# Attention keys in chunks of 128, 128, 128 and 64, the last chunk on quarters and eighths of TensorE

## The chip, the cores and the metric

One core of a Trainium2 chip. The metric is device time in microseconds (us), the median of a few runs; an interval is 95%. All runs told of here are at a granted TensorE clock of 0.988 to 0.998, where 1 is full speed. A ratio compares the mean times of two kernels' runs of the same rounds, so it isn't quite the ratio of the medians.

## The reference, cut to what matters

```python
# q, k, v: (8, 12, 448, 64) float32: 8 batches, 12 heads, 448 positions, 64 wide
q_n, k_n = rmsnorm(q, g_q), rmsnorm(k, g_k)
attn = softmax(q_n @ k_n.T / 8)            # 448 x 448 per head
x = (attn @ v)                             # -> (3584, 768)
h = x @ w_in                               # 768 -> 2048
out = (h - tanh(h)) @ w_out                # 2048 -> 768
```

The kernel works on pairs of heads: 48 pairs, six to a batch. The products with the weights of batch b run between the attention of batch b + 1, on the same TensorE. All matmuls are f32.

## The kernel before

Keys stand in four chunks of 112 rows. For each pair: turn k and q (transposes), scores with keys on the partitions (both heads together, 64 rows of the array each), exponentials into `p`, the column totals (a matmul with ones), values (`v` as weights, four column tiles of 32: two heads, two halves of the head's width), and the division by the totals.

```python
ps_s = pool("ps_s", bufs=5, space=PSUM)     # sc_bank(): five banks in turn
ps_m = pool("ps_m", bufs=3, space=PSUM)     # mm_bank(): three, for the products

def scores(s, half):                        # two of the four chunks
    ...
    nc.tensor.matmul(sc[:CP, :S], lhsT=kT[r, c * CP : (c + 1) * CP], rhs=qT[r, :], ...)
    ...
    nc.scalar.activation(p[:, h, i, :], tiles[h][:CP, :S], AF.Exp, ...)

def values(s, av):                          # one bank, 448 queries at a time
    for c in range(NCH):
        for m in range(2):
            for h in range(2):
                r = (2 * m + h) * BL
                nc.tensor.matmul(av[r : r + BL, :S], lhsT=v_nat[:, h, c, ...], rhs=p[:, h, c % 2, :], ...)

def slot(s):                                # one pair, from the second batch on
    gap = gap_ns(s)
    if s < 2 * NP:
        totals(s, sc_bank())
    scores(s + 1, 0); load(s + 2, "v")      # conditions cut
    run(gap)                                # products of the batch before
    turn(s + 2, sc_bank(), sc_bank()); squares(s + 3); load(s + 4, "kq")
    run(gap)
    if s >= 2 * NP:
        totals(s, sc_bank())
    divide(s, values(s, sc_bank()))         # division on VectorE
    scores(s + 1, 1); add(s + 1)
    norm(s + 3)
    run(gap)
    norm_q(s + 3)
    run(gap)
```

The pairs of batch 0 have slots of their own (`first_slot`), without products. In the first two batches weights are rounded too, much of it on VectorE.

Of the kernel before, what the change touches and what calls it, by code (L numbers as in the profile page):

```python
# [89 lines left out]
    nc.gpsimd.tensor_tensor(out=bits, in0=bits, in1=raw[:, :, 0], op=ALU.add)  # L90


def bounded_path(tc, ctx, q, k, v, moe_w_in, moe_w_out, out, g_col, ident, ones, neg_half):



# [29 lines left out]
    ORDER = (1, 5, 6, 2, 3, 7, 4)  # L126
    SLOTS, SLOT = 6, 8 * P
    BL = 32
    assert HS * 2 == S and HC * 2 == CD and SETS * 4 == CF and HC * P == HALF and S % BL == 0

    def pool(name, **kw):
        return ctx.enter_context(tc.tile_pool(name=name, **kw))
# [21 lines left out]
    def load(s, names):  # L154
        b, hp = steps[s]
        for name in names:
            src = {"q": q, "k": k, "v": v}[name]
            bufs = 3 if name == "v" else 2
            pair = src[b, 2 * hp : 2 * hp + 2].rearrange("h (p c) d -> p h c d", c=NCH)
            if name == "k":  # L160
                t = nat.tile([CP, NCH, 2, D], F32, name="k_nat", bufs=bufs)
                for h in range(2):
                    nc.sync.dma_start(out=t[:, :, h, :], in_=pair[:, h])
            else:
                t = nat.tile([CP, 2, NCH, D], F32, name=f"{name}_nat", bufs=bufs)
                nc.sync.dma_start(
                    out=t.rearrange("p h c d -> p h (c d)"), in_=pair.rearrange("p h c d -> p h (c d)")
                )
            loaded[name, s] = t


# [171 lines left out]

    def squares(s):
        n = nat.tile([CP, NCH, 2, D], F32, name="n", bufs=1)
        sq = nat.tile([CP, 2 * NCH, D], F32, name="sq", bufs=1), n.rearrange("p c h d -> p (c h) d")
        normed[s] = sq, n
        for i, name in ((1, "q"), (0, "k")):
            nc.scalar.activation(sq[i], loaded[name, s].rearrange("p a b d -> p (a b) d"), AF.Square)

    def norm(s):

        sq, n = normed[s]
        rr = small.tile([CP, 2, 2 * NCH], F32, name="rr", bufs=3)
        for group in ((1,), (0,)) if s < NP else ((0, 1),):
            for i in group:
                nc.vector.reduce_sum(rr[:, i], sq[i], axis=AX.X)  # L357
            r = rr[:, group[0] : group[-1] + 1].rearrange("p i r -> p (i r)")
            nc.vector.tensor_scalar(out=r, in0=r, scalar1=1.0 / D, scalar2=1e-6, op0=ALU.mult, op1=ALU.add)  # L359
            nc.gpsimd.tensor_tensor(out=r, in0=r, in1=neg_half[:, : r.shape[1]], op=ALU.pow)  # L360
        normed[s] = rr, n

    def norm_q(s):
        rr, n = normed[s]
        t = loaded.pop(("q", s))
        nc.vector.tensor_tensor(  # L366
            out=n.rearrange("p c h d -> p h c d"), in0=t,
            in1=rr[:, 1].rearrange("p (h c) -> p h c", h=2)[:, :, :, None].to_broadcast([CP, 2, NCH, D]),
            op=ALU.mult,
        )  # L370

    def turn(s, tk, tq):

        rr, n = normed.pop(s)
        kn = loaded.pop(("k", s))
        for c in range(NCH):
            nc.tensor.transpose(tk[:, c * CP : (c + 1) * CP], kn[:, c].rearrange("p h d -> p (h d)"), ident[:CP, :CP])  # L377
        kT = qkp.tile([P, S], F32, name="kT")
        nc.scalar.mul(kT, tk[:, :S], g_col)
        for c in range(NCH):  # L380
            nc.tensor.transpose(  # L381
                tq[:, c * CP : (c + 1) * CP], n[:, c].rearrange("p h d -> p (h d)"), ident[:CP, :CP]
            )
        qT = qkp.tile([P, S], F32, name="qT")
        nc.scalar.copy(out=qT, in_=tq[:, :S])
        turned[s] = rr, kT, qT

    def sc_bank():
        return ps_s.tile([P, 512], F32, name="sc")

    def scores(s, half):

        rr, kT, qT = turned[s]
        p = probs[s, half] = pp.tile([CP, 2, NCH // 2, S], F32, name="p")
        for i in range(NCH // 2):
            c = half * (NCH // 2) + i
            tiles = []
            for h in range(2):
                r = slice(h * D, (h + 1) * D)
                sc = sc_bank()  # L400
                nc.tensor.matmul(  # L401
                    sc[:CP, :S], lhsT=kT[r, c * CP : (c + 1) * CP], rhs=qT[r, :], start=True, stop=True
                )
                tiles.append(sc)
            for h in range(2):
                nc.scalar.activation(  # L406
                    p[:, h, i, :], tiles[h][:CP, :S], AF.Exp, scale=rr[:, 0, 2 * c + h : 2 * c + h + 1]
                )

    def add(s):  # L410

        if s <= NP + NP // 2:
            sums[s] = []
            return
        t = sp.tile([CP, 2, S], F32, name="sum")
        sums[s] = [t]
        parts = [probs[s, c // 2][:, :, c % 2, :] for c in range(NCH)]
        nc.vector.tensor_tensor(out=t, in0=parts[0], in1=parts[1], op=ALU.add)  # L418
        for part in parts[2:]:
            nc.vector.tensor_tensor(out=t, in0=t, in1=part, op=ALU.add)  # L420

    def values(s, av):
        v_nat = loaded.pop(("v", s))
        for c in range(NCH):
            p = probs[s, c // 2]
            for m in range(2):
                for h in range(2):
                    r = (2 * m + h) * BL
                    nc.tensor.matmul(  # L429
                        av[r : r + BL, :S], lhsT=v_nat[:, h, c, m * BL : (m + 1) * BL], rhs=p[:, h, c % 2, :],  # L430
                        start=(c == 0), stop=(c == NCH - 1),
                    )
        return av

    def totals(s, dn):

        t = sums.pop(s)
        parts = t if t else [probs[s, c // 2][:, :, c % 2, :] for c in range(NCH)]
        for i, p in enumerate(parts):
            for n in range(2):  # L440
                for h in range(2):
                    r = (2 * n + h) * BL
                    nc.tensor.matmul(  # L443
                        dn[r : r + BL, :HS], lhsT=ones[:CP, :BL], rhs=p[:, h, n * HS : (n + 1) * HS],
                        start=(i == 0), stop=(i == len(parts) - 1),
                    )
        rs = whole[s] = sp.tile([P, HS], F32, name="rs")
        nc.vector.reciprocal(rs, dn[:, :HS])  # L448

    def divide(s, av):  # L450
        b, hp = steps[s]
        rs = whole.pop(s)
        x = xT[b, hp] = xp.tile([P, S], F32, name="xT")
        for n in range(2):
            for m in range(2):
                nc.vector.tensor_tensor(  # L456
                    out=x[m * D : (m + 1) * D, n * HS : (n + 1) * HS],
                    in0=av[m * D : (m + 1) * D, n * HS : (n + 1) * HS], in1=rs[n * D : (n + 1) * D], op=ALU.mult,
                )
        del probs[s, 0], probs[s, 1]  # L460
        if hp < HC:
            return
        c = hp - HC
        if c == 0:
            tt[b] = tp.tile([P, 3, HC, HS], F32, name="tt", bufs=1)
        eng = nc.vector if b == 0 and c == HC - 1 else nc.gpsimd
        x11, x12, x21, x22 = (xT[b, r][:, n : n + HS] for r in (c, hp) for n in (0, HS))
        t1, t2, t4 = (tt[b][:, i, c] for i in range(3))
        eng.tensor_tensor(out=t1, in0=x12, in1=x11, op=ALU.subtract)
        eng.tensor_tensor(out=t2, in0=x22, in1=t1, op=ALU.subtract)  # L470
        eng.tensor_tensor(out=x12, in0=x22, in1=x12, op=ALU.subtract)
        eng.tensor_tensor(out=t4, in0=x21, in1=t2, op=ALU.subtract)
# [243 lines left out]
    def has(s):  # L716
        return 0 <= s < NS

    def first_slot(s):
# [13 lines left out]
        if has(s + 1):  # L733
            scores(s + 1, 1)
            add(s + 1)
        av = values(s, mm_bank()) if has(s) else None
        norm_q(s + 3)
        if has(s):
            divide(s, av)
# [3 lines left out]
    def slot(s):  # L743
# [12 lines left out]
        if has(s + 4):  # L756
            load(s + 4, "kq")
        run(gap)
        if s >= 2 * NP:
            totals(s, sc_bank())  # L760
        divide(s, values(s, sc_bank()))
        if has(s + 1):
            scores(s + 1, 1)
            add(s + 1)
# [21 lines left out]
def general_path(tc, ctx, q, k, v, moe_w_in, moe_w_out, out, g_col, ident, neg_half):  # L786
# [67 lines left out]
    def prep(s):  # L854

        for name in ("k", "q"):
# [7 lines left out]
            nc.vector.tensor_scalar(  # L864
                out=rr, in0=rr, scalar1=1.0 / D, scalar2=1e-6, op0=ALU.mult, op1=ALU.add
            )
            nc.gpsimd.tensor_tensor(out=rr, in0=rr, in1=neg_half[:, : 2 * NCH], op=ALU.pow)
            nc.vector.tensor_tensor(
                out=n.rearrange("p c h d -> p h c d"), in0=t,
                in1=rr.rearrange("p (h c) -> p h c", h=2)[:, :, :, None].to_broadcast([CP, 2, NCH, D]),  # L870
# [143 lines left out]
def kernel(  # L1014
# [44 lines left out]
    make_identity(nc, ident)  # L1059
    ones = consts.tile([P, D // 2], F32, name="ones")  # L1060
    nc.vector.memset(ones, 1.0)
    neg_half = consts.tile([CP, 4 * NCH], F32, name="neg_half")
    nc.vector.memset(neg_half, -0.5)
    bounded = nc.values_load(flag[0:1, 0:1])

    with tc.If(bounded) as cmp:
        with ExitStack() as arm, tc.manual_schedule():
            bounded_path(tc, arm, q, k, v, moe_w_in, moe_w_out, out, g_col, ident, ones, neg_half)
    with cmp.Else():
        with ExitStack() as arm:  # L1070
            general_path(tc, arm, q, k, v, moe_w_in, moe_w_out, out, g_col, ident, neg_half)
# [30 lines left out]
```

## Time and profile before

| | before |
|---|---|
| time, median of 3 runs | 1472.6 us (1471.8 to 1473.1) |
| TensorE busy | 1439.5 us, 98% |
| share of TensorE in the chain that ended last (followed back from the last instruction) | 89% |
| one steady pair, start of totals to start of totals | 29.27 us |

A busy TensorE isn't one at its peak. The space between the starts of single matmuls tells more, and the prediction below works from it; its lines are shown there.

### The profile page before, as it was taken

What the parts mean: (1) busy time and instruction counts of PE and PEld (TensorE: products, weight loads), DVE (VectorE), ACT (ScalarE), POOL (GpSimd) and SP (SyncE); (2) the same over time, 40 slices, a digit from 0 to 9 for tenths busy, and PEclk for the clock granted to TensorE, in tenths of its full rate; (3) what the DMA queues carried; (4) which work ended last, traced back from release to release, by engine and by line L of the source; (5) the groups of instructions that cost most, each with busy time, mean ns of one, the idle gap of its engine ahead of it and who ended that gap; (6) DMA issues with size and microseconds to landing.
All of it is one profiled execution on the core that took longest, in us unless ns stands there. A gap on an engine that the chain in (4) does not pass through costs nothing.

```text
span 1472.3 us, 22159 instructions
## 1 busy us (share of the span) xinstructions
PE 1439.5 (98%) x8544; PEld 1148.3 (78%) x8544; DVE 804.7 (55%) x1162; ACT 467.4 (32%) x850; POOL 510.0 (35%) x336
## 2 busy tenths in 40 slices
PE   6889999999999999999999999999999999999997
PEld 3357754588888888788878887888788878889997
DVE  4888987756534663456445554545554366433322
ACT  6755554233222333223322332223232233201100
POOL 4555665233421343224423233322342134312310
PEclk9999999999999999999999999999999999999999
DMA  9758788964466454644464546555545654555663
GB/s 186 154 155 221 240 257 215 247 193 140 138 176 182 135 175 132 193 138 155 150 185 135 167 131 189 146 131 173 170 147 140 183 163 136 146 163 157 184 195 97
DMA packets 244998, 247.33 MB, mean 168 GB/s; under 512 B 143380, under 2 KB 187156, under 8 KB 244884
## 3 DMA queue, kind: packets, MB, share of 16 engines
q1 hardware_dynamic: 244560, 245.82, 58.7%
q8 instruction: 70, 1.15, 0.3%
q14 instruction: 44, 0.36, 0.1%
q10 hardware_dynamic: 324, 0.00, 0.0%
HBM read 212.34 MB, written 33.42 MB: 167 GB/s over the span
## 4 chain that ended last, share of the span: by engine, by line
PE 89%; DVE 6%; DMA 3%; issue 1%; POOL 0%; SPq 0%; ACT 0%; ACTq 0%; DVEq 0%; POOLq 0%
PE mm L510 62%; PE sc L401 9%; PE sc L429 9%; PE mm L675 4%; PE sc L443 2%; DMA q_nat<-in_q_dram 1%; PE sc L381 1%; PE sc L377 1%; DMA w_raw<-in_moe_w_out_dram 1%; DVE sum L420 1%; DVE rr L357 1%; DVE xT L456 1%; PE mm L429 1%; DVE sum L418 0%; DMA gT<-in_moe_w_in_dram 0%
## 5 line engine op out<-in xcount | busy, mean ns | idle before, releaser
L406 ACT ACTIVATE p<-sc,rr 112x448 f32<-112x448 f32 x384 | 211.9, 636 | 473.7 <-PE sc L401 462.2
L510 PE MATMUL mm<-xT,w_f 128*128 128x224 f32 x1392 | 279.4, 355 | 0.9 <-DVE s L576 0.6
L510 PEld LDWEIGHTS mm<-xT,w_f 128*128 128x128 f32 x1392 | 259.8, 190 | 20.3 <-issue 11.3
L510 PEld LDWEIGHTS mm<-gT,w_f 128*128 128x128 f32 x1344 | 251.4, 190 | 23.4 <-issue 22.7
L510 PE MATMUL mm<-gT,w_f 128*128 128x224 f32 x1344 | 267.7, 355 | 0.0
L360 POOL TENSOR_TENSOR rr<-rr,neg_half 112x16 f32<-112x16 f32 (+1 forms) x54 | 146.4, 2715 | 317.6 <-DVE rr L359 311.1
L510 PE MATMUL mm<-tt,w_f 128*128 128x224 f32 x1044 | 211.3, 354 | 0.0
L510 PEld LDWEIGHTS mm<-tt,w_f 128*128 128x128 f32 x1044 | 196.1, 190 | 8.0 <-issue 8.0
L510 PE MATMUL mm<-tg,w_f 128*128 128x224 f32 x1008 | 200.4, 353 | 0.0
L510 PEld LDWEIGHTS mm<-tg,w_f 128*128 128x128 f32 x1008 | 189.5, 190 | 0.0
L401 PE MATMUL sc<-qT,kT 64*112 64x448 f32 x768 | 174.2, 566 | 1.3 <-ACT p L406 0.7
L547 POOL TENSOR_TENSOR gT<-s,th 128x448 f32<-128x448 f32 x96 | 119.6, 1255 | 150.5 <-ACT th L546 150.0
L470 POOL TENSOR_TENSOR tt<-xT,tt 128x224 f32<-128x224 f32 x23 | 32.4, 1410 | 346.8 <-DVE xT L456 346.7
L429 PE MATMUL sc<-p,v_nat 112*32 112x448 f32 x1344 | 135.4, 544 | 0.0
L401 PEld LDWEIGHTS sc<-qT,kT 64*112 64x112 f32 x768 | 63.1, 174 | 90.8 <-issue 79.2
L420 DVE TENSOR_TENSOR sum<-sum,p 112x896 f32<-112x896 f32 x76 | 93.8, 1235 | 7.9
L429 PEld LDWEIGHTS sc<-p,v_nat 112*32 112x32 f32 x1344 | 43.3, 111 | 70.3 <-issue 64.7
L456 DVE TENSOR_TENSOR xT<-sc,rs 64x224 f32<-64x224 f32 x168 | 65.2, 388 | 58.0 <-PE sc L429 54.3
L546 ACT ACTIVATE th<-s 128x448 f32<-128x448 f32 x96 | 55.2, 578 | 117.1 <-DVE s L576 65.0
L366 DVE TENSOR_TENSOR n<-q_nat,rr 112x512 f32<-112x512 f32 x48 | 53.3, 1110 | 69.7 <-POOL rr L360 68.8
L448 DVE RECIPROCAL rs<-sc 128x224 f32<-128x224 f32 x42 | 65.4, 1557 | 39.5 <-PE sc L443 39.4
L629 DVE TENSOR_TENSOR s<-mm,s 128x224 f32<-128x224 f32 x21 | 8.2, 391 | 132.0 <-PE mm L510 132.0
(97 smaller groups left out, 1385.1 us busy)
## 6 DMA issues: line engine op xcount, KB each, us to landing
w_f<-w_in SPq DMA_DIRECT2D x196, 384.0 KB, 3.7
w_f<-w_out SPq DMA_DIRECT2D x147, 512.0 KB, 4.6
w_raw<-in_moe_w_out_dram SPq DMA_DIRECT2D x16, 768.0 KB, 5.7
k_nat<-in_k_dram SPq DMA_DIRECT2D x96, 112.0 KB, 3.8
q_nat<-in_q_dram SPq DMA_DIRECT2D x48, 224.0 KB, 4.2
v_nat<-in_v_dram SPq DMA_DIRECT2D x48, 224.0 KB, 4.8
out_dram<-th SPq DMA_DIRECT2D x192, 56.0 KB, 1.9
w_in<-w_out SPq DMA_DIRECT2D x21, 384.0 KB, 6.9
```

What stands on the lines that cost most here:

```text
L360: nc.gpsimd.tensor_tensor(out=r, in0=r, in1=neg_half[:, : r.shape[1]], op=ALU.pow)
L366: nc.vector.tensor_tensor(out=n.rearrange("p c h d -> p h c d"), in0=t, in1=rr[:, 1].rearrange("p (h c) -> p h c", h=2)[:, :, :, None].to_ ...
L401: nc.tensor.matmul(sc[:CP, :S], lhsT=kT[r, c * CP : (c + 1) * CP], rhs=qT[r, :], start=True, stop=True)
L406: nc.scalar.activation(p[:, h, i, :], tiles[h][:CP, :S], AF.Exp, scale=rr[:, 0, 2 * c + h : 2 * c + h + 1])
L420: nc.vector.tensor_tensor(out=t, in0=t, in1=part, op=ALU.add)
L429: nc.tensor.matmul(av[r : r + BL, :S], lhsT=v_nat[:, h, c, m * BL : (m + 1) * BL], rhs=p[:, h, c % 2, :], start=(c == 0), stop=(c == NCH - 1),
L448: nc.vector.reciprocal(rs, dn[:, :HS])
L456: nc.vector.tensor_tensor(out=x[m * D : (m + 1) * D, n * HS : (n + 1) * HS], in0=av[m * D : (m + 1) * D, n * HS : (n + 1) * HS], in1=rs[n ...
L510: nc.tensor.matmul(bank[:, f * HS : (f + 1) * HS], lhsT=w[:, c * width + f, :], rhs=moving[p](c), start=(first and f == 0 and c == 0), sto ...
L546: nc.scalar.activation(th, h, AF.Tanh, bias=0.0, scale=1.0)
L547: eng.tensor_tensor(out=g[:, rows, cols], in0=h, in1=th, op=ALU.subtract)
L675: nc.tensor.matmul(bank[:, :S], lhsT=w_out_row(f, n // HC)[:, n % HC * P : (n % HC + 1) * P], rhs=g[:, f, :], start=(f == 0), stop=(f == C ...
```

## The change

Three chunks of 128 keys fill the array; the 64 keys left are loaded twice, on partitions 0 to 63 and 64 to 127. Their scores for the first half of the queries go to the lower partitions, for the second half to the upper (four 64x64 tiles together: quarters). Their values are eight 64x32 tiles (eighths). The prediction says why the two row halves get different PSUM banks (the buffers that TensorE writes to); so values use one bank for either half of the queries. The intent is fewer columns to stream: 3.5 chunks' worth in place of 4.

The core of the diff (loads, norms and `add` cut):

```diff
 def turn(s, tk, tq):
         for c in range(NCH):
-            nc.tensor.transpose(tk[:, c * CP : (c + 1) * CP], kn[:, c]..., ident[:CP, :CP])
+            rows = P if c < KF else KR
+            nc.tensor.transpose(tk[:, c * P : c * P + rows], kn[:rows, c]..., ident[:rows, :rows])
 def scores(s, half):
+            halves = 2 if c == KF else 1
+            keys, n = (P, S) if c < KF else (KR, HS)
+            for i in range(halves):
+                for h in range(2):
+                    nc.tensor.matmul(tiles[h][i * keys : (i + 1) * keys, :n], lhsT=kT[r, c * P : c * P + keys],
+                                     rhs=qT[r, i * n : (i + 1) * n], start=True, stop=True)
+def last_values(s, av):
+        for n in range(2):
+            keys = slice(n * KR, (n + 1) * KR)
+            ...
+                    nc.tensor.matmul(av[n][r : r + BL, :HS], lhsT=v_nat[keys, h, KF, ...],
+                                     rhs=p[keys, h, S:], start=True, stop=False)
 def values(s, av):
-                        av[r : r + BL, :S], lhsT=v_nat[:, h, c, ...], rhs=p[:, h, c % 2, :], ...
+        for n in range(2):
+            for c in range(KF):
+                            av[n][r : r + BL, :HS], lhsT=v_nat[:, h, c, ...],
+                            rhs=p[:, n * HS : (n + 1) * HS], start=False, stop=(c == KF - 1),
 def slot(s):
-        if s >= 2 * NP:
-            totals(s, sc_bank())
-        divide(s, values(s, sc_bank()))
+        dn = sc_bank() if s >= 2 * NP else None
+        av = [sc_bank() for _ in range(2)]
+        last_values(s, av)
+        if s >= 2 * NP:
+            totals(s, dn)
+        divide(s, values(s, av))
```

More of the change, by code (lines that the diff above doesn't have):

```diff
@@ L90, in round_weight_c, with bounded_path @@
     nc.gpsimd.tensor_tensor(out=bits, in0=bits, in1=raw[:, :, 0], op=ALU.add)
-def bounded_path(tc, ctx, q, k, v, moe_w_in, moe_w_out, out, g_col, ident, ones, neg_half):
+def bounded_path(tc, ctx, q, k, v, moe_w_in, moe_w_out, out, g_col, ident, ones, half_ones, neg_half):
     nc = tc.nc
@@ L128, in bounded_path @@
     BL = 32
-    assert HS * 2 == S and HC * 2 == CD and SETS * 4 == CF and HC * P == HALF and S % BL == 0
+    KF, KR = S // P, S % P
+    K0 = KF * P
+    assert HS * 2 == S and HC * 2 == CD and SETS * 4 == CF and HC * P == HALF and S % BL == 0 and 2 * KR == P and KF == NCH - 1 == 3
     def pool(name, **kw):
@@ L158, in load @@
             bufs = 3 if name == "v" else 2
-            pair = src[b, 2 * hp : 2 * hp + 2].rearrange("h (p c) d -> p h c d", c=NCH)
-            if name == "k":
-                t = nat.tile([CP, NCH, 2, D], F32, name="k_nat", bufs=bufs)
-                for h in range(2):
-                    nc.sync.dma_start(out=t[:, :, h, :], in_=pair[:, h])
-            else:
-                t = nat.tile([CP, 2, NCH, D], F32, name=f"{name}_nat", bufs=bufs)
-                nc.sync.dma_start(
-                    out=t.rearrange("p h c d -> p h (c d)"), in_=pair.rearrange("p h c d -> p h (c d)")
-                )
+            pair = src[b, 2 * hp : 2 * hp + 2]
+            if name == "q":
+                t = nat.tile([CP, 2, NCH, D], F32, name="q_nat", bufs=bufs)
+                nc.sync.dma_start(
+                    out=t.rearrange("p h c d -> p h (c d)"), in_=pair.rearrange("h (p c) d -> p h (c d)", c=NCH)
+                )
+            else:
+                full, rest = pair[:, :K0].rearrange("h (p c) d -> h p c d", c=KF), pair[:, K0:]
+                if name == "v":
+                    t = nat.tile([P, 2, NCH, D], F32, name="v_nat", bufs=bufs)
+                    last = t[:, :, KF]
+                    nc.sync.dma_start(
+                        out=t[:, :, :KF].rearrange("p h c d -> p h (c d)"), in_=full.rearrange("h p c d -> p h (c d)")
+                    )
+                else:
+                    t = nat.tile([P, NCH, 2, D], F32, name="k_nat", bufs=bufs)
+                    last = t[:, KF]
+                    for h in range(2):
+                        nc.sync.dma_start(out=t[:, :KF, h], in_=full[h])
+                for r in range(2):
+                    nc.sync.dma_start(out=last[r * KR : (r + 1) * KR], in_=rest.rearrange("h p d -> p h d"))
             loaded[name, s] = t
@@ L345, in squares @@
         n = nat.tile([CP, NCH, 2, D], F32, name="n", bufs=1)
-        sq = nat.tile([CP, 2 * NCH, D], F32, name="sq", bufs=1), n.rearrange("p c h d -> p (c h) d")
+        sq = nat.tile([P, 2 * NCH, D], F32, name="sq", bufs=1), n.rearrange("p c h d -> p (c h) d")
         normed[s] = sq, n
@@ L353, in norm @@
         sq, n = normed[s]
-        rr = small.tile([CP, 2, 2 * NCH], F32, name="rr", bufs=3)
-        for group in ((1,), (0,)) if s < NP else ((0, 1),):
-            for i in group:
-                nc.vector.reduce_sum(rr[:, i], sq[i], axis=AX.X)
-            r = rr[:, group[0] : group[-1] + 1].rearrange("p i r -> p (i r)")
+        rr = small.tile([P, 2, 2 * NCH], F32, name="rr", bufs=3)
+        for i, rows in ((1, CP), (0, P)):
+            r = rr[:rows, i]
+            nc.vector.reduce_sum(r, sq[i], axis=AX.X)
             nc.vector.tensor_scalar(out=r, in0=r, scalar1=1.0 / D, scalar2=1e-6, op0=ALU.mult, op1=ALU.add)
-            nc.gpsimd.tensor_tensor(out=r, in0=r, in1=neg_half[:, : r.shape[1]], op=ALU.pow)
+            nc.gpsimd.tensor_tensor(out=r, in0=r, in1=neg_half[:rows], op=ALU.pow)
         normed[s] = rr, n
@@ L367, in norm_q @@
             out=n.rearrange("p c h d -> p h c d"), in0=t,
-            in1=rr[:, 1].rearrange("p (h c) -> p h c", h=2)[:, :, :, None].to_broadcast([CP, 2, NCH, D]),
+            in1=rr[:CP, 1].rearrange("p (h c) -> p h c", h=2)[:, :, :, None].to_broadcast([CP, 2, NCH, D]),
             op=ALU.mult,
@@ L376, in turn @@
         for c in range(NCH):
-            nc.tensor.transpose(tk[:, c * CP : (c + 1) * CP], kn[:, c].rearrange("p h d -> p (h d)"), ident[:CP, :CP])
+            rows = P if c < KF else KR
+            nc.tensor.transpose(
+                tk[:, c * P : c * P + rows], kn[:rows, c].rearrange("p h d -> p (h d)"), ident[:rows, :rows]
+            )
         kT = qkp.tile([P, S], F32, name="kT")
@@ L393, in scores @@
         rr, kT, qT = turned[s]
-        p = probs[s, half] = pp.tile([CP, 2, NCH // 2, S], F32, name="p")
-        for i in range(NCH // 2):
-            c = half * (NCH // 2) + i
-            tiles = []
-            for h in range(2):
-                r = slice(h * D, (h + 1) * D)
-                sc = sc_bank()
-                nc.tensor.matmul(
-                    sc[:CP, :S], lhsT=kT[r, c * CP : (c + 1) * CP], rhs=qT[r, :], start=True, stop=True
-                )
-                tiles.append(sc)
-            for h in range(2):
+        if half == 0:
+            p = probs[s, 0] = pp.tile([P, 2, 2, S], F32, name="p", bufs=2)
+        else:
+            p = probs[s, 1] = pp.tile([P, 2, S + HS], F32, name="p_rest", bufs=1)
+        for c in (2 * half, 2 * half + 1):
+            tiles = [sc_bank() for _ in range(2)]
+            halves = 2 if c == KF else 1
+            keys, n = (P, S) if c < KF else (KR, HS)
+            for i in range(halves):
+                for h in range(2):
+                    r = slice(h * D, (h + 1) * D)
+                    nc.tensor.matmul(
+                        tiles[h][i * keys : (i + 1) * keys, :n], lhsT=kT[r, c * P : c * P + keys],
+                        rhs=qT[r, i * n : (i + 1) * n], start=True, stop=True,
+                    )
+            for h in range(2):
+                to = p[:, h, c] if half == 0 else p[:, h, :S] if c < KF else p[:, h, S:]
                 nc.scalar.activation(
-                    p[:, h, i, :], tiles[h][:CP, :S], AF.Exp, scale=rr[:, 0, 2 * c + h : 2 * c + h + 1]
+                    to, tiles[h][:, :n], AF.Exp, scale=rr[:, 0, 2 * c + h : 2 * c + h + 1]
                 )
@@ L414, in add @@
             return
-        t = sp.tile([CP, 2, S], F32, name="sum")
+        t = sp.tile([P, 2, S], F32, name="sum")
         sums[s] = [t]
-        parts = [probs[s, c // 2][:, :, c % 2, :] for c in range(NCH)]
-        nc.vector.tensor_tensor(out=t, in0=parts[0], in1=parts[1], op=ALU.add)
-        for part in parts[2:]:
-            nc.vector.tensor_tensor(out=t, in0=t, in1=part, op=ALU.add)
-    def values(s, av):
-        v_nat = loaded.pop(("v", s))
-        for c in range(NCH):
-            p = probs[s, c // 2]
+        p, rest = probs[s, 0], probs[s, 1]
+        nc.vector.tensor_tensor(out=t, in0=p[:, :, 0], in1=p[:, :, 1], op=ALU.add)
+        nc.vector.tensor_tensor(out=t, in0=t, in1=rest[:, :, :S], op=ALU.add)
+        for n in range(2):
+            part = t[n * KR : (n + 1) * KR, :, n * HS : (n + 1) * HS]
+            nc.vector.tensor_tensor(out=part, in0=part, in1=rest[n * KR : (n + 1) * KR, :, S:], op=ALU.add)
+    def last_values(s, av):
+        v_nat, p = loaded["v", s], probs[s, 1]
+        for n in range(2):
+            keys = slice(n * KR, (n + 1) * KR)
             for m in range(2):
@@ L429, in values @@
                     nc.tensor.matmul(
-                        av[r : r + BL, :S], lhsT=v_nat[:, h, c, m * BL : (m + 1) * BL], rhs=p[:, h, c % 2, :],
-                        start=(c == 0), stop=(c == NCH - 1),
-                    )
+                        av[n][r : r + BL, :HS], lhsT=v_nat[keys, h, KF, m * BL : (m + 1) * BL],
+                        rhs=p[keys, h, S:], start=True, stop=False,
+                    )
+    def values(s, av):
+        v_nat = loaded.pop(("v", s))
+        for n in range(2):
+            for c in range(KF):
+                for m in range(2):
+                    for h in range(2):
+                        r = (2 * m + h) * BL
+                        p = probs[s, 0][:, h, c] if c < 2 else probs[s, 1][:, h]
+                        nc.tensor.matmul(
+                            av[n][r : r + BL, :HS], lhsT=v_nat[:, h, c, m * BL : (m + 1) * BL],
+                            rhs=p[:, n * HS : (n + 1) * HS], start=False, stop=(c == KF - 1),
+                        )
         return av
     def totals(s, dn):
-        t = sums.pop(s)
-        parts = t if t else [probs[s, c // 2][:, :, c % 2, :] for c in range(NCH)]
-        for i, p in enumerate(parts):
+        parts = [t[:, h, n * HS : (n + 1) * HS] for t in sums.get(s, ()) for n in range(2) for h in range(2)]
+        parts = [(parts, [ones[:, :BL]] * 2)] if parts else []
+        if not sums.pop(s):
+            p, rest = probs[s, 0], probs[s, 1]
+            for full in (p[:, :, 0], p[:, :, 1], rest[:, :, :S]):
+                parts.append(
+                    ([full[:, h, n * HS : (n + 1) * HS] for n in range(2) for h in range(2)], [ones[:, :BL]] * 2)
+                )
+            parts.append(([rest[:, h, S:] for _ in range(2) for h in range(2)], [half_ones[:, n] for n in range(2)]))
+        for i, (moving, by) in enumerate(parts):
             for n in range(2):
@@ L443, in totals @@
                     nc.tensor.matmul(
-                        dn[r : r + BL, :HS], lhsT=ones[:CP, :BL], rhs=p[:, h, n * HS : (n + 1) * HS],
+                        dn[r : r + BL, :HS], lhsT=by[n], rhs=moving[2 * n + h],
                         start=(i == 0), stop=(i == len(parts) - 1),
@@ L457, in divide @@
                     out=x[m * D : (m + 1) * D, n * HS : (n + 1) * HS],
-                    in0=av[m * D : (m + 1) * D, n * HS : (n + 1) * HS], in1=rs[n * D : (n + 1) * D], op=ALU.mult,
+                    in0=av[n][m * D : (m + 1) * D, :HS], in1=rs[n * D : (n + 1) * D], op=ALU.mult,
                 )
@@ L735, in first_slot @@
             add(s + 1)
-        av = values(s, mm_bank()) if has(s) else None
+        if has(s):
+            av = [mm_bank() for _ in range(2)]
+            last_values(s, av)
+            values(s, av)
         norm_q(s + 3)
@@ L758, in slot @@
         run(gap)
+        dn = sc_bank() if s >= 2 * NP else None
+        av = [sc_bank() for _ in range(2)]
+        last_values(s, av)
         if s >= 2 * NP:
-            totals(s, sc_bank())
-        divide(s, values(s, sc_bank()))
+            totals(s, dn)
+        divide(s, values(s, av))
         if has(s + 1):
@@ L866, in prep @@
             )
-            nc.gpsimd.tensor_tensor(out=rr, in0=rr, in1=neg_half[:, : 2 * NCH], op=ALU.pow)
+            nc.gpsimd.tensor_tensor(out=rr, in0=rr, in1=neg_half[:CP], op=ALU.pow)
             nc.vector.tensor_tensor(
@@ L1061 @@
     nc.vector.memset(ones, 1.0)
-    neg_half = consts.tile([CP, 4 * NCH], F32, name="neg_half")
+    half_ones = consts.tile([P, 2, D // 2], F32, name="half_ones")
+    nc.vector.memset(half_ones, 0.0)
+    for i in range(2):
+        nc.vector.memset(half_ones[i * D : (i + 1) * D, i], 1.0)
+    neg_half = consts.tile([P, 2 * NCH], F32, name="neg_half")
     nc.vector.memset(neg_half, -0.5)
@@ L1067 @@
         with ExitStack() as arm, tc.manual_schedule():
-            bounded_path(tc, arm, q, k, v, moe_w_in, moe_w_out, out, g_col, ident, ones, neg_half)
+            bounded_path(tc, arm, q, k, v, moe_w_in, moe_w_out, out, g_col, ident, ones, half_ones, neg_half)
     with cmp.Else():
```

## The prediction

> **What bounds the kernel now.** I read the page first (busy shares, slices, the chain that ended last), then the timeline of one pair of heads in the steady part (857 to 890 us) for TensorE and for its weight loads, then the chain in order of time over the first 112 us.
>
> ```profile
> PE 1439.5 (98%) x8544; PEld 1148.3 (78%) x8544; DVE 804.7 (55%) x1162; ACT 467.4 (32%) x850; POOL 510.0 (35%) x336
> ...
> PE   6889999999999999999999999999999999999997
> ...
> PE 89%; DVE 6%; DMA 3%; issue 1%; POOL 0%; SPq 0%; ACT 0%; ACTq 0%; DVEq 0%; POOLq 0%
> PE mm L510 62%; PE sc L401 9%; PE sc L429 9%; PE mm L675 4%; PE sc L443 2%; DMA q_nat<-in_q_dram 1%; PE sc L381 1%; PE sc L377 1%; DMA w_raw<-in_moe_w_out_dram 1%; DVE sum L420 1%; DVE rr L357 1%; DVE xT L456 1%; PE mm L429 1%; DVE sum L418 0%; DMA gT<-in_moe_w_in_dram 0%
> ```
>
> TensorE is full from about 110 us on, and the chain is TensorE for 89% of the span. Scores (L401) and values (L429), which the change rewrites, are 9% and 10% of it. Only the first three slices have room. So what counts is TensorE's time per pair of heads, 48 times, and separately the start.
>
> The matmul rows of one pair, then the weight loads (start, length; brackets are idle time before):
>
> ```profile
> 857.33 0.59 PE L443 MATMUL sc<-sum,ones 112*32 112x224 f32 x8
> 857.73 3.19 PE L429 MATMUL sc<-p,v_nat 112*32 112x448 f32 x32
> 860.85 1.76 PE L401 MATMUL sc<-qT,kT 64*112 64x448 f32 x8
> 862.54 2.54 PE L510 MATMUL mm<-xT,w_f 128*128 128x224 f32 x12
> ...
> 880.42 0.55 PE L377 MATMUL sc<-ident,k_nat 112*128 112x112 f32 x4
> 880.81 0.55 PE L381 MATMUL sc<-ident,n 112*128 112x112 f32 x4
> ```
> ```profile
> 858.11 0.13 PEld L429 LDWEIGHTS sc<-p,v_nat 112*32 112x32 f32 x4 [0.24 <-issue]
> 858.48 0.13 PEld L429 LDWEIGHTS sc<-p,v_nat 112*32 112x32 f32 x4 [0.25 <-issue]
> ...
> 860.85 0.28 PEld L401 LDWEIGHTS sc<-qT,kT 64*112 64x112 f32 x4 [0.73 <-issue]
> 861.32 0.18 PEld L401 LDWEIGHTS sc<-qT,kT 64*112 64x112 f32 x2 [0.20 <-issue]
> 861.69 0.18 PEld L401 LDWEIGHTS sc<-qT,kT 64*112 64x112 f32 x2 [0.20 <-issue]
> ```
>
> Each f32 matmul is two records. The four column tiles of values load together, and the next four follow 0.375 us later: 448 columns cost 376 ns per group of tiles that run together, whatever their number; 224 columns cost 190 ns (L510 starts every 189 ns). But the blocks are longer than their groups. Values are 8 groups, 3.01 us, yet scores start 3.12 us after values did: 0.11 us extra. The first group of scores takes 0.47 us to the second, not 0.376: 0.09 extra. After the last scores group (start 862.07, plus 0.375) L510 starts 0.10 late, and its second record follows 0.29 later, not 0.19. Taking start to start over all such places, leaving a shape costs a median 95 ns after one tile, 99 after two, 116 after four, and the first group of the new shape is longer by 27 ns at 32 weight columns, 94 at 112, 107 at 128, 59 for the transposes. Between L510 and the transposes (both full 128x128 tiles) it is 2 ns.
>
> **What the Trainium skill says.** "TensorEngine Tiling (Array Packing)", Key Properties: changing the tiling mode, not just the tile, drains TensorE. The trace agrees: 95 to 116 ns at each change, 2 ns without one. "TensorE: Matmul & The Clock Gate", LDWEIGHTS (loading the stationary operand): a load costs its columns divided by 1.2 ns. 32, 112 and 128 give 27, 93 and 107: just the unhidden first load found above; 64 would give 53. The same page, Measured speedup vs the span model: tiles run together at about 4 ns per further tile, to 16 tiles. Here it is 6.5 ns for four; eight (64x32) are not in this trace. "TensorEngine Tiling (Array Packing)", Gotcha 1: PSUM Pressure: different row tiles must write different banks. That is why each half of the queries gets its own bank; nothing in the trace tests it.
>
> **The change part by part, per pair.** The built program gives scores of the last chunk 64x64 tiles, its values 64x32, and the transpose of the 64 last keys 64x128 where all eight transposes had 128x128. So the change adds three visits to new modes.
>
> Values: removed, 8 groups of 376 = 3008 ns. Added: 2 groups of 190 for the eighths (380), a mode change from 64x32 to 128x32 (95 plus 7 further tiles at 6.5, about 143, plus 27 for the load, 170), and 3 chunks x 2 halves x 2 = 12 groups of 190 (2280). Entry and exit stay. Sum 2830, that is -178 ns.
>
> Scores: removed, 2 groups of 376 (752). Added: 2 groups of 190 (380), a change from 64x128 to 64x64 (99 + 53 = 152), a dearer exit (116 for 99, +17), loads of 128 columns for 112 at both visits (2 x 13 = 26). Sum -177 ns.
>
> Turning k and q: 448 columns before and after for k, but one transpose is alone in a mode: in 95 + 59, out 95 + 59, +308 ns.
>
> Totals: four parts, or one, as before; 0. Sum per pair: -178 - 177 + 308 = -47 ns; times 48, -2.3 us. Without the mode changes it would have been -752 + 380 - 3008 + 2660 = -720 ns, or -34.6 us (2.3%), which I take for the intent.
>
> Off TensorE. ScalarE: two of eight exponentials halve, saved and hidden. VectorE: the third add (1235 ns) becomes two of 64x448, about 620 each from the 620 ns that a 448-column row takes: even. GpSimd: one pow of 112x16 (3017 ns) becomes two of eight columns (1658 each), but q's goes first, so q's is ready 1.4 us earlier, and one reduction (0.68) earlier too. DMA: four more issues per pair (two for k, two for v, at about 0.5 us of the queue) and 65 KB more; in the steady part weights are asked for five products ahead (five of 12 records at 0.19 us are 11.4 us) and land in 3.7 to 4.6 us, so this is hidden.
>
> The start (first 104 us, nine slots) is a mix:
>
> ```profile
> 5.51 3.24 DMA q_nat<-in_q_dram
> ...
> 39.35 1.69 PE mm L429 x16
> ...
> 41.59 1.68 ACT p L406 x3
> ...
> 77.02 2.91 POOL rr L360
> 81.10 0.14 issue
> 81.23 0.58 PE sc L381 x4
> ```
>
> The first q comes behind two more k transfers: +1.1 us. The queue issues back to back until about 35 us, with weights moving: about +2 us for the additional transfers. Second: here the scores of the next pair stand ahead of this pair's values, and their exponentials wait for a p buffer. Before, that buffer was read by the first half of values (the x16 above); now the one p_rest buffer is read until values end, so they start 1.1 us later, in six slots, and the next scores wait for their banks. ScalarE has about that much room per slot, so I book half: +3 us. Third, the shorter path through pow (the 2.91 above) gives back some 1.5 to 2 us in the two slots where TensorE waited: -3 us. Start: about +3 us.
>
> Total: 1472.6 - 2.3 + 3 = 1473 us.
>
> **The rivals.** (1) The mode changes are cheap: from 64x128 to 64x64 or from 64x32 to 128x32 only one side of the tile changes, and a lone transpose may hide its load. For: none of these pairs is in the trace. Against: every change that is there costs 95 or more, in the row and in the column direction alike. Without any, 1438 to 1441; without those of the transpose alone, 15 us less, 1458. (2) The eighths don't run together. If the two row halves took turns, 2 more groups of 190 per pair, +18 us: 1491. Against: the two row tiles of scores run together here, and so do four column tiles. (3) A wait for a PSUM bank: the last chunk's scores take banks of the totals and of the first half of values, so they wait for the reciprocal (1.56 us) and two divisions (0.39 each). By my count these end 2.5 us after the totals; values take until 2.3, and the chunk before another 0.95: free by some 0.7 us. If not, up to 1 us in 42 slots. (4) The start loses more than booked, as its queue is near full: up to +10 us.
>
> **Range and chances.** The steady sum is -17.0 us (two changes of mode inside) against +14.8 us (two more); a quarter off on one is 4 us, rival 1 in part is -15, rival 2 +18. So 1459 to 1488 should hold eight in ten. Faster by over 2% (under 1443) needs nearly every change to be free: 6%. Slower by 2% (over 1502) needs rivals 2 and 4, or bank waits: 6%. Within: 88%.
>
> **What would show it.** Right: values and eighths together about 2.7 us with a gap of 0.17 between eighths and totals; the 64-row transpose followed by a q transpose some 0.2 us later, not 0.1; from one steady pair to the next 29.2 us, as now (29.27: 857.33 to 886.60). Wrong: eighths' records spread over 0.76 us, not 0.38; idle time of TensorE in front of the last scores; pairs 0.3 us or more shorter than now; or the first L510, which starts at 91.4 us now, more than 10 us off that.

## The result, and the profile after

1483.2 us (1481.1 to 1488.1, four runs) against 1472.8 (four runs): ratio 1.0076, interval 1.005 to 1.010. The change is slower by 0.8%, clear of noise but under 2%. The range held it, the point was 10 us short.

A steady pair of the changed kernel, the matmul rows of its timeline (start, length):

```profile
868.82 0.61 PE L453 MATMUL sc<-p_rest,v_nat 64*32 64x224 f32 x16
869.36 0.59 PE L487 MATMUL sc<-sum,ones 128*32 128x224 f32 x8
869.77 0.94 PE L466 MATMUL sc<-p,v_nat 128*32 128x224 f32 x16
...
872.15 1.56 PE L421 MATMUL sc<-qT,kT 64*128 64x448 f32 x12
873.64 2.54 PE L554 MATMUL mm<-xT,w_f 128*128 128x224 f32 x12
...
891.54 0.69 PE L391 MATMUL sc<-ident,k_nat 128*128 128x128 f32 x4
892.16 0.60 PE L397 MATMUL sc<-ident,n 112*128 112x112 f32 x4
892.60 2.45 PE L554 MATMUL mm<-xT,w_f 128*128 128x224 f32 x12
...
898.01 0.61 PE L453 MATMUL sc<-p_rest,v_nat 64*32 64x224 f32 x16
```

The eighths (L453) take 0.54 us to the start of totals: two groups of 190 and 0.16 of mode change, so all eight tiles do run together. Turning k and q takes 1.06 us (891.54 to 892.60), where it took 0.77 before (880.42 to 881.19, in the prediction). From pair to pair it is 29.19 us (868.82 to 898.01), for 29.27 before. So the steady part is a little faster, as forecast, and can't be where 10 us went.

Two stretches of time, from:to, length, then busy time and instructions (x) of TensorE, its weight loads, VectorE, ScalarE and GpSimd, then clock and DMA; before first, then after:

```profile
104.00:300.00 196.00, 193.49 (x996) 122.78 (x1000) 161.67 (x214) 86.75 (x140) 101.97 (x54) 0.98 0.81 230
300.00:1326.00 1026.00, 1025.12 (x6168) 846.30 (x6164) 530.25 (x764) 295.34 (x559) 328.85 (x222) 1.00 0.53 157
```
```profile
104.00:300.00 196.00, 184.56 (x1136) 118.44 (x1136) 160.51 (x220) 81.81 (x134) 101.52 (x60) 0.97 0.78 221
300.00:1326.00 1026.00, 1024.52 (x7430) 874.21 (x7427) 534.04 (x833) 288.34 (x569) 326.81 (x255) 1.00 0.55 159
```

Between 104 and 300 us, where batch 1's attention and batch 0's products run, TensorE idles for 11.4 us after the change (196.00 less 184.56) and idled for 2.5 before (a wait of 3.1 us that ended at 104.65 falls mostly outside of this stretch). To place the loss, take the start of each pair's turn (its first k transpose) in both traces:

| turn of pair (from 0) | before, us | after, us | later by |
|---|---|---|---|
| 6 | 63.28 | 71.42 | 8.1 |
| 8 | 96.83 | 99.31 | 2.5 |
| 10 | 164.10 | 166.48 | 2.4 |
| 11 | 197.09 | 205.52 | 8.4 |
| 13 | 262.31 | 274.92 | 12.6 |
| 47 | 1261.74 | 1271.92 | 10.2 |

The start gives 2.5 us net, two steps at 182 and 252 us (and one at 114, made up for by a shorter wait nearby) give 10 more, and the other 34 pairs win back 2.4. At the first of the two steps, TensorE and VectorE of the changed kernel show this:

```profile
175.41 0.56 PE L466 MATMUL sc<-p_rest,v_nat 128*32 128x224 f32 x8
175.90 1.54 PE L421 MATMUL sc<-qT,kT 64*128 64x448 f32 x6
182.31 1.02 PE L421 MATMUL sc<-qT,kT 64*64 64x224 f32 x6 [4.87 <-DVE xT L500]
183.26 3.35 PE L554 MATMUL mm<-tt,w_out 128*128 128x224 f32 x8
```
```profile
176.52 0.96 DVE L82 SCALAR_TENSOR_TENSOR w_out<-w_raw,w_out 128x768 int32<-128x768 int32 x1
177.40 0.62 DVE L610 TENSOR_TENSOR s<-mm,s 128x448 f32<-128x448 f32 x1
177.93 1.93 DVE L78 TENSOR_SCALAR w_out<-w_out 128x768 f32<-128x768 f32 x1
179.89 0.56 DVE L79 TENSOR_SCALAR w_out<-w_out 128x768 int32<-128x768 int32 x1
180.49 0.96 DVE L82 SCALAR_TENSOR_TENSOR w_out<-w_raw,w_out 128x768 int32<-128x768 int32 x1
181.36 1.64 DVE L500 TENSOR_TENSOR xT<-sc,rs 64x224 f32<-64x224 f32 x4
```

Values ended near 175.8. The last of the quarters (L421, 64*64) wait 4.87 us for the divisions (L500), which stand behind weight rounding in VectorE's queue (L78, L79, L82). The five score banks go round: after two banks for values, the last chunk's second bank is the one that holds the first half of values. Before, the last scores of these slots needed only the bank of the turned q (in steady pairs, that of totals). And the products after the wait (L554, eight records in 3.35 us) start 0.376 us apart for about ten records, where they take 0.189: TensorE runs at half rate after the idle time, which costs 1.9 us more. The two other waits, also followed by half rate:

```profile
114.27 0.60 PE L421 MATMUL sc<-qT,kT 64*64 64x224 f32 x6 [2.66 <-DVE xT L500]
```
```profile
252.21 1.02 PE L421 MATMUL sc<-qT,kT 64*64 64x224 f32 x6 [2.84 <-DVE xT L500]
```

### The profile page after: what moved, and what is told of

It is laid out like the page before. It is cut to its first block, busy times and chain, and to the rows that moved or that the text cites. A ratio compares the mean times of both kernels' runs of the same rounds, so it can differ in the third digit from the quotient of the medians.

```text
span 1481.9 us, 26026 instructions
## 1 busy us (share of the span) xinstructions
PE 1443.6 (97%) x10272; PEld 1186.5 (80%) x10272; DVE 808.4 (55%) x1245; ACT 450.7 (30%) x850; POOL 508.6 (34%) x378
## 4 chain that ended last, share of the span: by engine, by line
PE 88%; DVE 7%; DMA 2%; SPq 1%; issue 1%; ACT 0%; POOL 0%; ACTq 0%; DVEq 0%; POOLq 0%
PE mm L554 62%; PE sc L421 9%; PE sc L466 5%; PE mm L719 5%; PE sc L487 2%; PE sc L397 1%; PE sc L453 1%; PE sc L391 1%; DVE xT L500 1%; DVE rs L492 1%; DMA gT<-in_moe_w_in_dram 1%; DVE rr L371 1%; DVE w_out L289 1%; SPq L182 1%; DVE sum L443 1%
## 5 line engine op out<-in xcount | busy, mean ns | idle before, releaser
L554 PE MATMUL mm<-xT,w_f 128*128 128x224 f32 x1392 | 279.4, 355 | 1.5 <-DVE s L620 1.5
L554 PEld LDWEIGHTS mm<-xT,w_f 128*128 128x128 f32 x1392 | 259.8, 190 | 16.3 <-issue 9.5
L554 PE MATMUL mm<-gT,w_f 128*128 128x224 f32 x1344 | 267.7, 355 | 0.0
L373 POOL TENSOR_TENSOR rr<-rr,neg_half 112x8 f32<-112x8 f32 x96 | 157.8, 1666 | 316.6 <-DVE rr L372 310.6
L554 PEld LDWEIGHTS mm<-gT,w_f 128*128 128x128 f32 x1344 | 251.4, 190 | 17.1 <-DVE th L649 7.2
L554 PE MATMUL mm<-tt,w_f 128*128 128x224 f32 x1044 | 211.2, 354 | 0.0
L554 PEld LDWEIGHTS mm<-tt,w_f 128*128 128x128 f32 x1044 | 196.1, 190 | 5.9 <-issue 5.9
L554 PE MATMUL mm<-tg,w_f 128*128 128x224 f32 x1008 | 200.4, 353 | 0.0
L554 PEld LDWEIGHTS mm<-tg,w_f 128*128 128x128 f32 x1008 | 189.5, 190 | 0.0
L421 PE MATMUL sc<-qT,kT 64*128 64x448 f32 (+1 forms) x960 | 171.6, 502 | 13.9 <-DVE xT L500 10.4
L427 ACT ACTIVATE p_rest<-sc,rr 128x448 f32<-128x448 f32 x192 | 88.3, 541 | 282.2 <-PE sc L421 265.9
L591 POOL TENSOR_TENSOR gT<-s,th 128x448 f32<-128x448 f32 x96 | 112.8, 1182 | 159.4 <-ACT th L590 159.4
L427 ACT ACTIVATE p<-sc,rr 128x448 f32<-128x448 f32 x192 | 106.0, 639 | 200.2 <-PE sc L421 200.1
L421 PEld LDWEIGHTS sc<-qT,kT 64*128 64x128 f32 (+1 forms) x960 | 62.2, 166 | 99.3 <-issue 59.2
L466 PE MATMUL sc<-p,v_nat 128*32 128x224 f32 x1344 | 79.1, 353 | 0.0
L719 PE MATMUL mm<-gT,w_out 128*128 128x448 f32 x192 | 75.5, 549 | 0.0
L500 DVE TENSOR_TENSOR xT<-sc,rs 64x224 f32<-64x224 f32 x168 | 65.3, 389 | 8.6 <-PE sc L466 1.2
L719 PEld LDWEIGHTS mm<-gT,w_out 128*128 128x128 f32 x192 | 36.3, 193 | 36.3 <-issue 34.8
```

The source lines that it names most:

```text
L373: nc.gpsimd.tensor_tensor(out=r, in0=r, in1=neg_half[:rows], op=ALU.pow)
L421: nc.tensor.matmul(tiles[h][i * keys : (i + 1) * keys, :n], lhsT=kT[r, c * P : c * P + keys], rhs=qT[r, i * n : (i + 1) * n], start=True, ...
L427: nc.scalar.activation(to, tiles[h][:, :n], AF.Exp, scale=rr[:, 0, 2 * c + h : 2 * c + h + 1])
L466: nc.tensor.matmul(av[n][r : r + BL, :HS], lhsT=v_nat[:, h, c, m * BL : (m + 1) * BL], rhs=p[:, n * HS : (n + 1) * HS], start=False, stop= ...
L500: nc.vector.tensor_tensor(out=x[m * D : (m + 1) * D, n * HS : (n + 1) * HS], in0=av[n][m * D : (m + 1) * D, :HS], in1=rs[n * D : (n + 1) * ...
L554: nc.tensor.matmul(bank[:, f * HS : (f + 1) * HS], lhsT=w[:, c * width + f, :], rhs=moving[p](c), start=(first and f == 0 and c == 0), sto ...
```

## The experiments

**turn128 and late, one edit each; both together.** Two theories for the loss (the modes and the bank wait), each with an edit that takes one away:

```diff
 # turn128: the last keys as a full block, their second copy with them
-            rows = P if c < KF else KR
+            rows = P
```
```diff
 # late: in the slots of batch 1, the last scores one gap later
         divide(s, values(s, av))
-        if has(s + 1):
+        if s >= 2 * NP and has(s + 1):
             scores(s + 1, 1)
             add(s + 1)
         if has(s + 3):
             norm(s + 3)
         run(gap)
+        if s < 2 * NP:
+            scores(s + 1, 1)
+            add(s + 1)
```

> The changed kernel with the last 64 keys turned as a full block of 128 rows (their second copy with them), so that no transpose stands in a 64x128 tile. Theory (each lone mode change costs what the trace shows: 96 ns to enter, 149 to leave, 58 on the next transpose, against 53 ns for 64 more columns): 0.24 us less per pair of heads, 11.7 us in all, about 1471.5 us; steady pairs 28.95 us apart instead of 29.19. Rival (the lone transpose hides in the queue, the 10 us come from elsewhere): 1483 us, pairs unchanged.

Measured: 1473.5 us (ratio to before 1.0005, interval 0.9985 to 1.0026), 9.7 less than the changed kernel. The turn in its timeline:

```profile
885.11 0.60 PE L391 MATMUL sc<-ident,k_nat 128*128 128x128 f32 x4
885.55 0.55 PE L397 MATMUL sc<-ident,n 112*128 112x112 f32 x4
885.93 2.45 PE L554 MATMUL mm<-xT,w_f 128*128 128x224 f32 x12
```

0.82 us in place of 1.06, with 64 columns more. That is the 0.24 of the theory; from pair 13 to pair 47 the distance to the changed kernel grows by 8.2 us, 0.24 a pair. In the first two batches it gains only 1.4 us of the 3.1 that 13 pairs would give: there, part of it only lengthens waits. The bank waits (2.7, 5.1 and 3.3 us) are still there. So one transpose in a mode of its own costs a quarter of a microsecond.

> The changed kernel with the second half of the scores one gap later in the six slots of the first batch that still round weights, so that TensorE has products to do while VectorE gets to the divisions. Theory (the 10 us come from the last scores waiting there for the bank that the divisions free: 2.8, 4.9 and 2.8 us of idle time and the half clock after them): 8 to 11 us less, 1472 to 1475 us, and no idle time over 1 us in front of the last scores. Rival (VectorE's weight work bounds these slots, so the wait only moves to another instruction): within 3 us of 1483.

Measured: 1470.5 us (0.9984 of before, interval 0.9967 to 1.0001), 12.7 less than the changed kernel, a little more than expected. Between 104 and 300 us its granted clock is 1.00, where it was 0.97 in the changed kernel: the half rate went with the waits. Its timeline in the same place:

```profile
170.09 0.56 PE L466 MATMUL sc<-p_rest,v_nat 128*32 128x224 f32 x8
170.58 1.78 PE L554 MATMUL mm<-tt,w_out 128*128 128x224 f32 x8
172.20 3.95 PE L554 MATMUL mm<-xT,w_out 128*128 128x224 f32 x20
176.07 1.56 PE L421 MATMUL sc<-qT,kT 64*128 64x448 f32 x12
177.57 1.02 PE L554 MATMUL mm<-xT,w_out 128*128 128x224 f32 x4
180.10 2.54 PE L554 MATMUL mm<-xT,w_out 128*128 128x224 f32 x12 [1.51 <-DVE s L612]
```

Products fill the time until VectorE has divided, and nothing waits in front of the scores. A wait of 1.5 us for VectorE at a product is left, as the kernel before had one of 1.5 us there (182.89). VectorE does not bound these slots.

> The changed kernel with both edits, the full transpose and the later scores. Theory: the two gains add up, 1483 - 11.7 - 9 = 1462 us, faster than the kernel before by 0.7%. Rival (they share a bound in the first batch): 1468 us or more.

Measured: 1460.4 us (0.9916 of before, interval 0.990 to 0.993). The two gains add up (9.7 + 12.7 = 22.4 of them expected from 1483.2, 22.8 found), and the layout with both edits beats the kernel before by 0.8%. In its trace 10.4 us of that come between pair 13 and pair 47, 0.31 a pair. Not all of the rest need belong to the layout: norms apart, which it contains, give 0.2% alone (beforesplit, below).

**bank: the wait added to the kernel before.** Values in two banks, one for each half of the output rows; the matmuls are the same:

```diff
-                        av[r : r + BL, :S], lhsT=v_nat[...], rhs=p[:, h, c % 2, :],
+                        av[m][r : r + BL, :S], lhsT=v_nat[...], rhs=p[:, h, c % 2, :],
 ...
-        divide(s, values(s, sc_bank()))
+        divide(s, values(s, [sc_bank(), sc_bank()]))
```

(The divisions go by `m` first, so that the first bank comes free early.)

> The kernel before with values in two banks (one for each half of the output rows), all matmuls the same, so that the last scores take the bank that the divisions free. Theory (the bank wait alone costs the 10 us): 1480 to 1484 us, idle time of 2 to 5 us in front of the last scores in three slots between 104 and 300 us. Rival (the loss belongs to the new layout, its DMAs or modes): 1473 us.

Measured: 1498.5 us (1.0177 of before, interval 1.016 to 1.019): more than expected. The waits stand in the same three places: 2.2, 4.8 and 5.3 us. By pair 13 the kernel is 17.5 us behind; 3.0 of them arose in the start, before any slot with two banks, where this trace shows half rate from 80.9 to 87.5 us. The rest is a surprise in the steady part, 0.21 us a pair. Its scores there, then VectorE:

```profile
879.28 3.19 PE L429 MATMUL sc<-p,v_nat 112*32 112x448 f32 x32
882.40 2.05 PE L401 MATMUL sc<-qT,kT 64*112 64x448 f32 x8
```
```profile
879.53 1.56 DVE L448 RECIPROCAL rs<-sc 128x224 f32<-128x224 f32 x1
882.53 1.63 DVE L456 TENSOR_TENSOR xT<-sc,rs 64x224 f32<-64x224 f32 x4 [1.44 <-PE sc L429]
```

The scores take 2.05 us, 1.76 before: here both banks are filled until values end, so the divisions start at 882.53 and the last scores wait for two of them. In the changed kernel one bank has all of its queries early:

```profile
870.02 1.56 DVE L492 RECIPROCAL rs<-sc 128x224 f32<-128x224 f32 x1 [0.46 <-PE sc L487]
871.68 1.65 DVE L500 TENSOR_TENSOR xT<-sc,rs 64x224 f32<-64x224 f32 x4
```

Values run there until about 872.0, and the divisions start before that, right after the reciprocal. So, by these two traces, splitting values by queries keeps the second bank from costing anything in steady pairs; no run tests that alone. The run does show that the second bank by itself makes the waits of batch 1.

**beforelate: is the later order just a better order?**

```diff
 # the kernel before
         divide(s, values(s, sc_bank()))
-        if has(s + 1):
+        if s >= 2 * NP and has(s + 1):
             scores(s + 1, 1)
 ...
+        if s < 2 * NP:
+            scores(s + 1, 1)
+            add(s + 1)
```

> The kernel before with the same later scores in six slots. Theory (the edit pays in the changed kernel only because it takes the bank wait away, which the kernel before doesn't have): within 3 us of before, 1470 to 1476 us. Rival (later scores help any kernel in these slots, because VectorE's weight work holds other things too): 1461 to 1466 us, and then the layout with the full transpose isn't what beats the kernel before.

Measured: 1474.2 us against 1474.6 (ratio 1.0006, interval 0.999 to 1.002). It gives nothing where there is no bank wait to take away. Its trace adds a warning about the half rate. The kernel before, then this one, after the same wait at the start of batch 1:

```profile
104.65 3.35 PE L510 MATMUL mm<-xT,w_out 128*128 128x224 f32 x8 [3.09 <-DVE s L566]
```
```profile
104.50 1.78 PE L510 MATMUL mm<-xT,w_out 128*128 128x224 f32 x8 [3.08 <-DVE s L566]
```

The same eight records take 3.35 us in one and 1.78 in the other. So a wait of 3.1 us is followed by half rate in one execution and not in another, and a single trace can be some 2 us off for that alone.

**The start: beforedma and beforesplit.** Two parts of the change put alone into the kernel before: more transfers, and norms of q and k apart.

```diff
 # beforedma: same bytes, two more transfers for k and two for v
-                    nc.sync.dma_start(out=t[:, :, h, :], in_=pair[:, h])
+                    nc.sync.dma_start(out=t[:, :3, h, :], in_=pair[:, h, :3])
+                for h in range(2):
+                    nc.sync.dma_start(out=t[:, 3:, h, :], in_=pair[:, h, 3:])
 # (v likewise: three chunks in one, the fourth by head)
 # beforesplit
-        for group in ((1,), (0,)) if s < NP else ((0, 1),):
+        for group in ((1,), (0,)):
```

> The kernel before with k loaded by four transfers and v by three, the same bytes. Theory (the additional issues put the start back and are hidden later): +1 to +3 us at the first batch, 1474 to 1476 us. Rival (transfers matter in the steady part too): more, growing with each pair; or (they never matter): 1473 us.

Measured: 1475.1 us (ratio 1.0012, interval 0.9995 to 1.0029), inside the noise as a whole. At the start the trace shows it: the fourth q is asked for at 27.1 us in place of 24.5 and the first product comes at 93.7 in place of 91.4 (93.9 in the changed kernel). About half of these 2.3 us are made up soon (1.1 are left at pair 9, 1.2 at pair 47). It does not grow with the pairs.

> The kernel before with the norm of q and of k always apart, as the changed kernel has it. Theory (q's power is ready earlier, which took some 3 us out of the start at the two places where TensorE waited for it): 1469.5 to 1471.5 us. Rival (the wait is for something else there): 1473 us.

Measured: 1470.4 us (0.9981, interval 0.9965 to 0.9998). The first product comes at 88.3 us, 3.1 earlier. GpSimd's pow (L360) and q's transposes (L381) before, then with the norms apart:

```profile
77.02 2.90 POOL L360 TENSOR_TENSOR rr<-rr,neg_half 112x16 f32<-112x16 f32 x1 [2.36 <-DVE rr L359]
81.23 0.58 PE L381 MATMUL sc<-ident,n 112*128 112x112 f32 x4 [1.94 <-DVE n L366]
```
```profile
73.59 3.24 POOL L360 TENSOR_TENSOR rr<-rr,neg_half 112x8 f32<-112x8 f32 x2 [1.77 <-DVE rr L359]
76.52 0.57 PE L381 MATMUL sc<-ident,n 112*128 112x112 f32 x4 [2.72 <-DVE n L366]
```

q's transposes started 4.2 us after the start of the pow, and start 2.9 after it now. (The profiled execution is the fastest of the four: 1467.6 us, the others 1470.1 to 1471.5.) This is a gain that needs no part of the new layout.

**bothorder: the wait for the single p_rest buffer.** In the first slots, with both edits in, values come ahead of the next pair's last scores:

```diff
-        if has(s + 1):
-            scores(s + 1, 1)
-            add(s + 1)
         if has(s):
             av = [mm_bank() for _ in range(2)]
             last_values(s, av)
             values(s, av)
+        if has(s + 1):
+            scores(s + 1, 1)
+            add(s + 1)
```

> The changed kernel with both edits, and in the first slots values ahead of the next pair's last scores. Theory (the single p_rest buffer makes ScalarE wait for values to end, and the scores behind it for their banks, some 3 us over six slots): 1457 to 1458 us. Rival (the start is bound by transfers and by VectorE): 1460 us or more.

Measured: 1460.8 us (both: 1460.4), the first product at 91.2 us (both: 91.4). This order doesn't pay. But it doesn't settle the theory, since it moves the wait and hardly shortens it: in the first 104 us ScalarE waits 14.6 us in front of p_rest for values in both, and 12.7 us for the scores, which now stand behind values, in bothorder. Two buffers for p_rest, which would have tried it directly, did not fit in memory, so no run shows what they would give.

## Why the prediction was right or wrong

*The steady part: right, term by term.* Leaving the eighths' mode costs 139 + 26 ns (forecast 143 + 27). Entering the quarters costs 99 and 53 more on the first group (99 + 53); leaving them 112 (116). Entering the lone transpose's mode costs 96, leaving it 149 (its own weight load counted in), and 58 more on the next, 303 together (308). Eight tiles run together. Per pair -0.08 us (-0.05). One reading off TensorE was too low, and hidden: the two short adds on VectorE take 0.79 us each on the mean (0.62). Run turn128 confirms the largest of the terms by taking it away. So rivals 1 (cheap mode changes) and 2 (eighths that take turns) are out: the first by the trace and turn128, the second by the trace.

*The bank wait: the step that failed.* Rival 3 was worked out for the steady pairs only ("free by some 0.7 us"), and there it holds. What it left out are the six slots of batch 1, where VectorE's queue holds weight rounding ahead of the divisions, so that at the largest of the waits they come 5.5 us after values end, not before. The forecast booked 0 for this. The trace shows 10.4 us of waits in three slots, and half-rate time after each; net of what the kernel before loses to waits there, 10 us. Runs late, bank and beforelate show from three sides that the second bank of values is the cause. This term is the 10 us that the point was short. Of the prediction's signs of being wrong it is the one that came: idle time of TensorE in front of the last scores.

*The start: near in sum, one term not confirmed.* Forecast +3, found +2.5 at the first product (93.9 us, before 91.4). But run late, whose code is the same up to there, has it at 92.4, so two traces of the same start differ by 1.5 us. Transfers: +2.3 (forecast +3.1). Norms apart: -3.1 (forecast -3). The +3 for the p_rest buffer is neither confirmed nor refuted: bothorder only moved the wait. Transfers and norms alone come to -0.8, so about 3.3 us at the start stay open. The record holds a lead: beforedma asks for the fourth q at 27.1 us, the changed kernel only at 29.4, with the first two transfers of k taking the queue 1.34 us to issue where beforedma's take 0.90. So beforedma, with the same number of transfers, takes in only part of their cost.

*The chances.* The case for slower by 2% named bank waits, and they came, but in three slots instead of in all of them. That the range reached to 1488 was owed to rival 2, which did not come; that it held 1483 is in part luck.

## What to carry to other kernels

Count the array's modes, not only its columns: in these traces each visit to another tile shape cost some 95 ns or more and a first weight load, so padding a lone small transpose to the full block can be cheaper than doing less of it. When a change needs one more buffer of a ring, go through every phase of the kernel and ask what stands in the queue of the engine that frees it; a margin worked out in the steady phase says nothing of the phase in which that engine has other work. Work to fill the wait with, moved in front of the waiting instruction, may cost nothing (beforelate: 1.0006).

## What the Trainium skill lacked or had wrong

- "TensorEngine Tiling (Array Packing)", Key Properties, says that a change of mode drains TensorE, but gives no cost. Here it is 95 ns after one tile, 99 after two, 112 to 116 after four, 139 after eight (near to 95 and 6.5 for each further tile), and then a weight load that nothing hides: 26 ns at 32 columns, 53 at 64, 107 at 128.
- No page says outright that a lone transpose of 64 rows is such a change; it made each pair 0.24 us longer than a transpose of 128 rows does (turn128).
- "TensorE: Matmul & The Clock Gate", LDWEIGHTS, gives columns over 1.2 for a load. That holds for the matmuls here, but the formula makes no exception for transposes, and a transpose with 128 columns to load adds 58 ns in its place, not 107.
- The same page, Measured speedup vs the span model, has about 4 ns for each further tile; here it is 6.5 ns, for four tiles and for eight.
- No page that I read warns that the second bank which tiles in different rows need is one more place of a ring, to be freed by another engine: run bank, which adds it alone, is 25 us slower (3.0 of them from the start of its trace).
